# Attention into a gated FFN on one core: one query group's x turned on TensorE, and unread identity products ahead of the first scores

## The chip, the cores and the metric

The kernel runs on one core of a Trainium2 chip. The metric is the device time of one execution in microseconds. The profile is of one execution, taken by the hardware profiler; its engines are named PE (TensorE), PEld (TensorE's weight loads), DVE (VectorE), ACT (ScalarE), POOL (GpSimd) and SP (SyncE, which here only issues DMAs).

## The reference

Eight batches, eight heads, 576 tokens of 64 elements a head, and 16 "beacon" keys and values ahead of each head's own. Attention is causal over the tokens and open to the beacons; its output, with the heads side by side, is the x (4608 tokens by 512) of a gated feed-forward layer.

```python
k_all = np.concatenate([beacon_k, k], axis=2)
v_all = np.concatenate([beacon_v, v], axis=2)
scores = scale * np.matmul(q, k_all.transpose(0, 1, 3, 2))   # causal mask on the tokens
a = np.exp(scores - scores.max(-1, keepdims=True))
a /= a.sum(-1, keepdims=True) + 1e-09
x = np.matmul(a, v_all)          # then (batch, token, head * 64): 4608 x 512
gate = np.maximum(x @ w_gate, 0.0)                           # 512 -> 1536
return (gate * (x @ w_val)) @ w_out                          # 1536 -> 512
```

## The kernel before, in words

**Attention.** A unit of attention is one batch, one pair of heads (four pairs) and one of two query groups: group 0 is the first 368 tokens in three query tiles (112, 128, 128 rows), group 1 the last 208 in two (128, 80). For a unit TensorE makes the scores with keys on the partitions (`qk`, L339; from batch 2 on in slabs over several units, L362), ScalarE takes the exponential (L388; slabs L370 and L372), VectorE multiplies the diagonal blocks with a triangular mask (L400; slabs L379 and L382; GpSimd does it for two units of the very start, L397). `av` (L421) multiplies the weights with v, which carries a column of ones, so that the sum of the weights comes along; VectorE takes the reciprocal (L429) and writes the divided x in bf16, tokens on the partitions (L430).

**Turning.** The FFN needs x with its features on the partitions (`xT`). There are two ways. `x_turn` (L437) issues DMA transposes on SP, one for each query tile, over all four pairs of a group, after the last pair's `av`. `x_turn_pair` (L445, L446) transposes one pair on TensorE, one product with the identity per query tile, into a PSUM bank, and an engine copies the bank into `xT`. Before the change, `x_turn_pair` serves batch 0 alone; batches 1 to 7 use `x_turn`. q and k are turned likewise: for batches 0 and 1 on TensorE (`pair_turn`, L319 and L322, copied out at L325; the beacons' keys at L290), from batch 2 on by DMA transposes on SP (L296), after a load on SP (L254, L255 and their like) and a cast to bf16 on GpSimd (L282). The program puts such a turn behind the next load or two: load at one step, cast two steps on, turn three steps on.

**FFN.** Tokens go in tiles of 368 and 208 (the query groups). For each tile, 12 units `ffn_up`: four products with a block of w_gate (L454), a Relu on ScalarE (L457), four products with a block of w_val (L462), and VectorE's product of the two (L470, `hT`). For each 128 tokens of a finished block of 512, a unit `ffn_down`: 12 products with w_out (L493), a copy on ScalarE (L498), and a store issued by GpSimd (L500).

**Order.** The program is written out by hand, engine by engine in the order of its text; semaphores alone tie the engines together. The start (batch 0's group 0) is spelled out: six small loads of q and k by GpSimd's queue (`cs`), then for each pair `pair_turn`, then `scores` (that is `start`, `qk`, `softmax`), with masks, weight loads (`chunk`, three pieces of w_gate and w_val, L554) and `av` between. From batch 1 on, a loop over steps takes a step's attention units and fills in FFN units up to a budget; the order of FFN units comes from a planner's costs and from when a tile's x is due. In a step, `aver` issues the `av` of the units of the step before, and `passed` issues loads, casts and turns whose time has come; `held` keeps these back while a group's last `av` has not been issued, so that `x_turn`'s transposes stand ahead of them on SP. Each of SP, GpSimd and the compute engines works strictly in its order, so an instruction that waits holds up all behind it.

**PSUM.** Two score tiles take four of the eight banks. The other four form the ring `f`: every other use of PSUM (transposes, `av`, FFN) takes the next bank in turn, and waits until its reader of four uses ago is done.

Of the kernel before, what the change touches and what calls it, by code (L numbers as in the profile page):

```python
# [10 lines left out]
FP32 = mybir.dt.float32  # L11
# [131 lines left out]
def kernel(  # L143
# [15 lines left out]
    P = 128  # L159
# [13 lines left out]
    V, G, A, T = nc.vector, nc.gpsimd, nc.scalar, nc.tensor  # L173

    const = ctx.enter_context(tc.tile_pool(name="const", bufs=1))
    ident = const.tile([P, P], BF16, name="ident")
# [34 lines left out]
    f_ps = Ring("f_ps", 4, space=bass.MemoryType.PSUM)  # L211
# [98 lines left out]
    def pair_turn(c, b, p, part, cps):  # L310
        r0, r1, s0 = PARTS[part]
        n = r1 - r0
        tps = [f_ps.tile([P, n, D], BF16, name="f") for _ in range(2)]
        for r in range(r0, r1):
            for i in range(2):
                rows = slice(i * D, (i + 1) * D)
                if isinstance(c, Load):
                    flat = c.c.rearrange("p a n -> p (a n)")
                    T.transpose(tps[i][:, r - r0], flat[rows, r * P:(r + 1) * P], ident[rows, rows])  # L319
                    continue  # L320
                for a in range(2):
                    T.transpose(tps[i][a * D:(a + 1) * D, r - r0], c[rows, 2 * p + a, r * D:(r + 1) * D],  # L322
                                ident[rows, rows])
        for i in range(2):
            cps[i](kqs[b % 2][:, i, p, Nb + s0:Nb + s0 + n * D].rearrange("q (p r) -> q p r", r=n),  # L325
                   tps[i].rearrange("q r p -> q p r"))
# [4 lines left out]
    def qk(u):  # L331
        u.s, u.p, u.parts = [], [], []
        kq = kqs[u.b % 2]
        for segs, cols, _ in SLABS[u.g]:
            s = s_ps.tile([P, 2, 512], FP32, name="s")
            for (kt, q0, n, c) in segs:
                for a in range(2):
                    rows = slice(a * D, (a + 1) * D)
                    T.matmul(s[:, a, c:c + n], kq[rows, 0, u.pi, kt * P:(kt + 1) * P],  # L339
                             kq[rows, 1, u.pi, Nb + q0:Nb + q0 + n], start=True, stop=True)  # L340
            u.s.append(s)
# [7 lines left out]
    class Slab:  # L349
# [26 lines left out]
        def mask(self):  # L376
            n, m = self.spans
            if n == 1:
                V.tensor_mul(self.p[:, :, :m], self.p[:, :, :m], tri[:, :, :m])  # L379
                return  # L380
            d = self.p.rearrange("p a (s c) -> p (a s) c", s=n)[:, :, :m]
            V.tensor_mul(d, d, tri[:, 0:1, :m].to_broadcast([P, 2 * n, m]))  # L382

    def softmax(u, which=(0, 1)):
        for i in which:
            cols = SLABS[u.g][i][1]
            flat, p = weights(cols)
            A.activation(p, u.s[i][:, :, :cols], AF.Exp, scale=scale)  # L388
            u.p.append(p)
            u.parts.append((flat, cols, SLABS[u.g][i][0]))  # L390
# [43 lines left out]
    def x_turn(u):  # L434
        for qi in QGROUPS[u.g]:
            r0, rn = QROWS[qi]
            nc.sync.dma_start_transpose(xT[:, :, u.b * S + r0:u.b * S + r0 + rn], u.x[:rn, qi, :])  # L437

    def x_turn_pair(u, cp):
        qt = QGROUPS[u.g]  # L440
        c0, c1 = QROWS[qt[0]][0], QROWS[qt[-1]][0] + QROWS[qt[-1]][1]
        tp = f_ps.tile([P, 384], BF16, name="f")
        for qi in qt:
            r0, rn = QROWS[qi]
            T.transpose(tp[:, r0 - c0:r0 - c0 + rn], u.x[:rn, qi, u.pi * P:(u.pi + 1) * P], ident[:rn, :rn])  # L445
        cp(xT[:, u.pi, u.b * S + c0:u.b * S + c1], tp[:, :c1 - c0])  # L446
# [78 lines left out]
    with tc.manual_schedule():  # L525
# [13 lines left out]
        for b in range(B):  # L539
            for p, g in [(p, g) for g in range(2) for p in range(NP)]:  # L540
                u = Burst()
# [3 lines left out]
        def start(u):  # L545
            if u.b not in xs:
                xs[u.b] = xsb.tile([P, NKT, d_model], BF16, name="x")
            u.x = xs[u.b]
# [10 lines left out]

        VV = (V.tensor_copy, V.tensor_copy)  # L560
        VA = (V.tensor_copy, A.copy)
        def scores(u):
            start(u)
            qk(u)
            softmax(u)

# [6 lines left out]
        for p in range(1, NP):  # L573
# [3 lines left out]
        G.affine_select(out=tri[:, :, P:], in_=tri[:, :, P:], pattern=[[0, 2], [1, 240 - P]],  # L577
                        compare_op=ALU.is_ge, fill=0.0, base=Nb, channel_multiplier=-1)

        first.cast(V, A)  # L580
        bk[0].cast(A)
        pair_turn(first, 0, 0, 0, VA)
        bk[0].turn(V.tensor_copy)
        pair_turn(c0, 0, 1, 0, VA)
        g0 = bursts[:NP]
        scores(g0[0])
        mask(g0[0], True)
        chunk(0, 256)
# [28 lines left out]
        ffn = []  # L617
# [7 lines left out]
        def next_ffn(mid=None):  # L625
            ffn.pop(0)[1](mid)
# [35 lines left out]
        while len(ffn) > LEFT:  # L662
            if len(ffn) == LEFT + 1:
                bk[1].turn(V.tensor_copy)
                pair_turn(c1, 1, 0, 2, VA)
            next_ffn()
# [46 lines left out]
        def budget(s):  # L713
            best = W0 if s < 8 else CAP * widths[s]
            for r in sorted(set(ready.values())):
                if r > pos[s]:
                    best = min(best, sum(c for c, _, e in ffn if ready[e] < r) / (r - pos[s]) * widths[s])
            return best

        clock = []  # L720

        def passed(t):
            while clock and clock[0][0] <= t + 1e-6:
                clock.pop(0)[2]()
# [18 lines left out]
        for s, e in enumerate(steps):  # L743
            units = [u for u in last if last[u] == s - 1]
            want += budget(s)

            def fits():
                return ffn and ready[ffn[0][2]] <= pos[s] and spent + ffn[0][0] / 2 <= want

            def held():  # L750
                return any(u.last for u in units)

            def aver():
                if units:
                    u = units.pop(0)
                    av(u)
                    if u.last:
                        x_turn(u)

            if not isinstance(e, list):  # L760
                u = e
                turn = u and u.b == 1 and u.g == 0 and not u.last
                if turn:
                    pair_turn(c1, 1, u.pi + 1, 2, VA)
                late = False
                if u:
                    late = not turn and ffn and ready[ffn[0][2]] <= pos[s] and ffn[0][0] < 1
                    start(u)
                    qk(u)
                    softmax(u, (0,) if late else (0, 1))  # L770
                while units:
                    aver()
                passed(pos[s])
                rest = []
                if late:
                    rest = [lambda: (softmax(u, (1,)), mask(u, which=(0,))), lambda: mask(u, which=(1,))]
                elif u:
                    mask(u)
                while fits():
                    spent += ffn[0][0]  # L780
                    next_ffn()
                    if rest:
                        rest.pop(0)()
                for f in rest:
                    f()
                continue
            for i, sl in enumerate(e):
                for u, _ in sl.segs:
                    start(u)
                sl.qk([f_ps.tile([P, 512], FP32, name="f") for _ in range(2)] if i == 0 else  # L790
                      s_ps.tile([P, 2, 512], FP32, name="s"))
            exps, masks = list(e), []

            def exp():
                if exps:
                    sl = exps.pop(0)
                    sl.exp()
                    masks.append(sl)

            exp()  # L800
            aver()
            if not held():
                passed(pos[s])
            gone, was, room = 0.0, spent, max(want - spent, 0.1)
            while fits():
                c = ffn[0][0]
                gone += c
                mid = gone >= STEP
                if mid:
                    gone = 0.0  # L810
                old = len(masks)
                next_ffn(exp if mid else None)
                spent += c
                if old:
                    masks.pop(0).mask()
                if mid:
                    aver()
                if not held():
                    passed(pos[s] + widths[s] * min((spent - was) / room, 0.99))
            while exps:  # L820
                exp()
            while units:
                aver()
            for sl in masks:
                sl.mask()
        assert not clock
        while ffn:
            if len(ffn) == 10:
                range_flags()
# [38 lines left out]
```

## Time and profile before

| | |
|---|---|
| Time, median of 4 runs | 377.61 us (376.09 to 378.18) |
| The profiled execution's own time | 375.27 us |
| Its span, first to last instruction | 373.5 us |
| TensorE busy / ScalarE / VectorE / GpSimd | 95% / 55% / 51% / 24% |
| DMA transposes of x on SP | 35, median 3.3 us from issue to landing |
| TensorE transposes of x (L445) | 20 |
| Copies of turned x (L446) | 4 on ScalarE (368 columns), 4 on VectorE (208 columns) |

Spans are of one execution, and the numbers that a view gives are of that one; the median belongs to other executions of the same kernel. In a timeline a line gives the start, the time from the start of the first to the end of the last instruction merged into it, engine, line, operation, output<-input, shape and count, and in brackets the idle time of the engine before it with what ended it. Products overlap: their pace is read from start to start, not from the length of one. "DMA xT<-x" names the landing of a transfer. In a wait list the three numbers are the total, the times and the longest.

### The profile page before, as it was taken

Reading aid. Unit: us, or ns where it says so; the run is one execution under the profiler, and the core shown is the slowest. Engines: PE = TensorE matmul, PEld = TensorE weight load, DVE = VectorE, ACT = ScalarE, POOL = GpSimd, SP = SyncE. Lnnn points to the kernel's source line nnn. Section 1 sums busy time; section 2 is a strip of 40 time slices with the busy share of each in tenths; the row PEclk is TensorE's granted clock in tenths of the full one; section 3 lists DMA queues with packets and bytes.
Section 4 is the critical chain, followed back from the end, with each engine's and each line's share of the span. In section 5 each row is a group of like instructions: output and inputs, shape, how many; then the busy total and the mean of one; then the engine's idle time right before and its main releaser. Section 6 shows DMA issues by size and latency. Waiting matters only on the chain.

```text
span 373.5 us, 9601 instructions
## 1 busy us (share of the span) xinstructions
PE 356.5 (95%) x3757; PEld 238.3 (64%) x3757; DVE 190.7 (51%) x630; ACT 204.3 (55%) x388; POOL 89.3 (24%) x126
## 2 busy tenths in 40 slices
PE   3799989999998999999999999999999999999995
PEld 2556666567745686565596657865596647865763
DVE  3657367457424674365365643564566625552230
ACT  5665366656555664555466554655565736632322
POOL 6962033321142112311321323111321011000100
PEclk9999999999999999999999999999999999999999
DMA  8999999999999887975868969878685021101202
GB/s 150 188 202 207 212 205 193 194 194 127 161 221 194 154 153 133 212 169 97 211 138 147 157 148 236 127 164 158 155 143 100 16 65 65 35 16 38 84 32 90
DMA packets 156947, 53.12 MB, mean 142 GB/s; under 512 B 146528, under 2 KB 154464, under 8 KB 156896
## 3 DMA queue, kind: packets, MB, share of 16 engines
q1 hardware_dynamic: 145088, 36.72, 56.5%
q0 software_dynamic: 11376, 15.27, 18.9%
q8 instruction: 31, 0.51, 0.6%
q10 hardware_dynamic: 432, 0.46, 0.4%
q14 instruction: 20, 0.16, 0.2%
HBM read 38.47 MB, written 9.44 MB: 128 GB/s over the span
## 4 chain that ended last, share of the span: by engine, by line
PE 87%; DMA 4%; SPq 2%; ACT 2%; DVE 1%; POOL 1%; issue 1%; POOLq 0%; ACTq 0%; DVEq 0%
PE f L454 24%; PE f L462 24%; PE f L493 22%; PE f L421 9%; PE s L362 3%; PE f L362 2%; PE s L339 2%; DMA cs<-in_q_dram 2%; DMA stg<-in_q_dram 2%; DMA kq<-c 1%; SPq L296 1%; POOL cs L308 1%; ACT p L388 1%; PE f L481 1%; DVE hT L470 1%
## 5 line engine op out<-in xcount | busy, mean ns | idle before, releaser
L470 DVE TENSOR_TENSOR hT<-g,f 128x208 bf16<-128x208 f32 (+14 forms) x288 | 92.8, 351 | 86.8 <-PE f L462 54.7
L454 PE MATMUL f<-xT,wg 128*128 128x368 bf16 (+1 forms) x768 | 125.9, 286 | 1.6 <-DMA xT<-x 1.0
L462 PE MATMUL f<-xT,wv 128*128 128x368 bf16 (+1 forms) x768 | 125.6, 286 | 0.9 <-DVE hT L470 0.8
L457 ACT ACTIVATE g<-f 128x368 f32<-128x368 f32 (+1 forms) x192 | 78.9, 414 | 78.5 <-PE f L454 41.9
L493 PE MATMUL f<-wo,hT 128*128 128x512 bf16 x420 | 94.7, 379 | 0.1
L462 PEld LDWEIGHTS <-wv 128*128 128x128 bf16 x768 | 71.0, 98 | 26.0 <-DVE hT L470 1.1
L454 PEld LDWEIGHTS <-wg 128*128 128x128 bf16 x768 | 69.6, 98 | 23.0 <-issue 3.3
L493 PEld LDWEIGHTS <-hT 128*128 128x128 bf16 x420 | 39.9, 98 | 44.2
L498 ACT COPY ob<-f 128x512 f32<-128x512 f32 x35 | 20.5, 585 | 65.5 <-PE f L493 57.8
L372 ACT ACTIVATE p<-s 128x992 bf16<-128x992 f32 (+2 forms) x56 | 53.8, 966 | 0.0
L282 POOL CAST c<-stg 128x1024 bf16<-128x1024 f32 (+1 forms) x30 | 31.2, 1041 | 88.9 <-DMA stg<-in_q_dram 86.3
L500 POOL DMA_DIRECT2D out_dram<-ob x32 | 17.3, 542 | 132.5 <-ACT ob L498 123.3
L429 DVE RECIPROCAL rall<-f 128x2 f32<-128x2 f32 (+1 forms) x96 | 16.6, 173 | 63.3 <-PE f L421 62.5
L421 PEld LDWEIGHTS <-p 128*128 128x128 bf16 (+2 forms) x960 | 36.1, 101 | 10.6 <-issue 6.2
L421 PE MATMUL f<-vx,p 128*128 128x65 bf16 (+2 forms) x960 | 41.5, 197 | 0.8 <-DVE p L400 0.8
L430 DVE TENSOR_TENSOR x<-f,rall 128x128 bf16<-128x128 f32 (+1 forms) x96 | 36.3, 378 | 3.5
L370 ACT ACTIVATE p<-f 128x496 bf16<-128x496 f32 (+2 forms) x56 | 28.7, 567 | 7.6 <-PE f L362 7.6
L388 ACT ACTIVATE p<-s 128x992 bf16<-128x992 f32 (+2 forms) x32 | 26.1, 867 | 5.0 <-PE s L339 4.9
L379 DVE TENSOR_TENSOR p<-p,tri 128x160 bf16<-128x160 bf16 (+1 forms) x72 | 28.6, 401 | 0.4 <-ACT p L372 0.4
L269 POOL CAST vx<-stg 128x1024 bf16<-128x1024 f32 (+2 forms) x21 | 18.9, 899 | 30.2 <-DMA stg<-in_v_dram 14.8
L362 PEld LDWEIGHTS <-kq 64*128 64x128 bf16 x384 | 13.9, 94 | 10.5 <-issue 9.4
L362 PE MATMUL s<-kq 64*128 64x208 bf16 (+4 forms) x256 | 16.2, 249 | 0.7 <-DMA kq<-c 0.7
(58 smaller groups left out, 108.9 us busy)
## 6 DMA issues: line engine op xcount, KB each, us to landing
out_dram<-ob POOLq DMA_DIRECT2D x32, 256.0 KB, 3.2
stg<-in_v_dram SPq DMA_DIRECT2D x24, 256.0 KB, 5.3
stg<-in_k_dram SPq DMA_DIRECT2D x18, 256.0 KB, 4.2
stg<-in_q_dram SPq DMA_DIRECT2D x18, 256.0 KB, 5.0
stg<-in_v_dram SPq DMA_DIRECT2D x8, 224.0 KB, 4.2
wo<-in_moe_w_out_dram POOLq DMA_DIRECT2D x3, 512.0 KB, 14.1
stg<-in_k_dram SPq DMA_DIRECT2D x6, 224.0 KB, 3.9
stg<-in_q_dram SPq DMA_DIRECT2D x6, 224.0 KB, 4.4
```

The costliest lines, as they stand in the source:

```text
L282: cp(self.c[:n], self.st[:n])
L362: T.matmul(o[:, c:c + n], kq[rows, 0, u.pi, kt * P:(kt + 1) * P], kq[rows, 1, u.pi, Nb + q0:Nb + q0 + n], start=True, stop=True)
L370: A.activation(p[:, a], self.s[a][:, :self.cols], AF.Exp, scale=scale)
L372: A.activation(p, self.s[:, :, :self.cols], AF.Exp, scale=scale)
L388: A.activation(p, u.s[i][:, :, :cols], AF.Exp, scale=scale)
L421: T.matmul(o[:m, j, a, 0:D + 1], p[:kr, c:c + m], vs[u.b % 2][:kr, kt, 2 * u.pi + a, 0:D + 1], start=first, stop=(kt == kts[-1]), skip_gro ...
L430: V.tensor_mul(u.x[:m, i0:i0 + j1 - j0, u.pi * P:(u.pi + 1) * P].rearrange("p j (a d) -> p j a d", a=2), o[:m, j0:j1, :, 0:D], r.unsqueeze ...
L454: T.matmul(g[:, :mn], wg[:, ki, nf * P:(nf + 1) * P], xT[:, ki, m0:m0 + mn], start=(ki == 0), stop=(ki == KM - 1))
L457: A.activation(gs[:, :mn], g[:, :mn], AF.Relu)
L462: T.matmul(u[:, :mn], wv[:, ki, nf * P:(nf + 1) * P], xT[:, ki, m0:m0 + mn], start=(ki == 0), stop=(ki == KM - 1))
L470: V.tensor_mul(hbs[i][:, nf, c - i * HB:e - i * HB], gs[:, c - m0:e - m0], u[:, c - m0:e - m0])
L493: T.matmul(o, hbs[i][:, nf, ms * P:(ms + 1) * P], wo[:, nf, :], start=(nf == 0), stop=(nf == NF - 1))
```

## The change

Two things are added. First, a function `keep_busy` that makes n products of the 128x128 identity with itself into one bank of the ring `f`, which nothing reads: 30 of them ahead of the first transposes, and 8 ahead of the scores of each of pairs 1, 2 and 3 of batch 0's group 0. Second, x of batch 2's group 0 is turned pair by pair by `x_turn_pair` with VectorE's copy, in place of the three DMA transposes of `x_turn`: a pair is noted after its `av`, and turned once two FFN units have been issued after that.

```diff
+        def keep_busy(n):
+            ps = f_ps.tile([P, P], FP32, name="f")
+            for _ in range(n):
+                T.matmul(ps, ident, ident, start=True, stop=True)
+
         def scores(u):
             start(u)
+            if u.g == 0 and u.pi:
+                keep_busy(8)
             qk(u)
             softmax(u)
...
+        keep_busy(30)
         first.cast(V, A)
         bk[0].cast(A)
         pair_turn(first, 0, 0, 0, VA)
...
-        clock = []
+        clock, unturned = [], []
...
+            def turn_pair():
+                if unturned and unturned[0][1] > len(ffn) + 1:
+                    x_turn_pair(unturned.pop(0)[0], V.tensor_copy)
+
...
                     av(u)
-                    if u.last:
+                    if (u.b, u.g) == (2, 0):
+                        unturned.append((u, len(ffn)))
+                    elif u.last:
                         x_turn(u)
...
                 next_ffn(exp if mid else None)
+                turn_pair()
                 spent += c
...
-        assert not clock
+        assert not clock and not unturned
```

In the built program TensorE gets 54 identity products and 12 transposes more, VectorE 4 copies of 368 columns more (the first two behind the second and the fourth FFN unit after the first pair's `av`, the last between the two `ffn_down` units ahead of the tile that reads it), and SP three DMA transposes less. Nothing else changes its place on any engine.

## The prediction

> **What bounds the kernel now.** I read the page first, then what TensorE waited for, then its timeline where those waits lie, then SP's queue and GpSimd over the same microseconds.
>
> The page's first lines:
>
> ```profile
> span 373.5 us, 9601 instructions
> PE 356.5 (95%) x3757; PEld 238.3 (64%) x3757; DVE 190.7 (51%) x630; ACT 204.3 (55%) x388; POOL 89.3 (24%) x126
> ```
>
> TensorE is busy 95% of the span, 17.0 us short of it. An edit gains only by shortening TensorE's work or by closing one of its gaps, and adds its own TensorE time in full wherever TensorE is otherwise dense. TensorE's waits (total us, times, longest us):
>
> ```profile
> PE f L319 <- ACT c L279: 5.6, 1, 5.6
> PE s L339 <- ACT p L388: 1.3, 2, 0.9
> PE f L454 <- DMA xT<-x: 1.0, 1, 1.0
> PE f L322 <- DMA cs<-in_q_dram: 0.8, 1, 0.8
> PE s L362 <- DMA kq<-c: 0.7, 1, 0.7
> ```
>
> First, second and fourth lie before 14 us, where the products go. The third is the one place where an x tile comes too late from the DMA transposes. TensorE's timeline there (start, us, instruction, idle before it):
>
> ```profile
> 106.51 5.34 PE L493 MATMUL f<-wo,hT 128*128 128x512 bf16 x24
> 112.90 0.78 PE L454 MATMUL f<-xT,wg 128*128 128x368 bf16 x4 [1.05 <-DMA xT<-x]
> ...
> 116.76 0.44 PE L362 MATMUL s<-kq 64*128 64x128 bf16 x4 [0.71 <-DMA kq<-c]
> ```
>
> Batch 2's first 368 tokens begin at 112.90 after 1.05 us idle; 3 us later the scores of batch 3 wait 0.71 us for kq. SP's queue, and the cast that the later kq needs:
>
> ```profile
> 101.25 3.04 SPq L296 DMA_TRANSPOSE kq<-c  x2
> ...
> 105.75 5.24 SPq L437 DMA_TRANSPOSE xT<-x  x3
> 111.10 2.53 SPq L296 DMA_TRANSPOSE kq<-c  x2
> ```
>
> ```profile
> 103.00 1.04 POOL L282 CAST c<-stg 128x1024 bf16<-128x1024 f32 x1 [3.06 <-DMA stg<-in_q_dram]
> ```
>
> SP issues in program order. Counting casts and turns in the program, the pair at 111.10 reads the tile cast at 103.00 to 104.04: it was ready 7 us earlier and stood behind the three x transposes. (The chain of waits says otherwise: it goes from 116.76 through the cast at 110.73. That cast feeds the next pair, at 115.79; I take the program's order over that inference.) So x's 5.24 us on SP cause both waits, 1.05 + 0.71 = 1.76 us.
>
> **The turns, TensorE.** Twelve transposes, 368 columns a pair. Nearest row: the two at 32.03 (128 + 80 columns) let the next product start at 32.13, so 0.10 us for 208 columns, 0.18 for 368, 0.71 for four pairs. Three pairs stand among dense products, the last between two down products (L493) ahead of 112; all 0.71 is paid. The Trainium skill speaks against this: "TensorE: Matmul & The Clock Gate", section "Part 4: PE-mode transpose", gives about 275 ns for one 128x128 transpose inside a kernel. Twelve of those make 3.3 us, more than the 1.76 us to be won, and the edit would lose 1.5. But that is one's duration (here too a record lasts some 0.26 us); in a stream the row's 0.05 us each counts. I take 0.71; ends 0.6 and 3.3, near the first.
>
> **The turns, VectorE and the ring.** Four copies of 368 columns out of PSUM; 208 columns took 0.26 (32.80), so about 0.45 each. The last two fall where VectorE idles over 2 us and cost nothing. The first two stand in its queue between the hT products (L470) of 90 to 94 us; there VectorE is busy 3.69 of 4.50 us. Behind them wait the division of the next pair's x and the hT products that free banks of the four-bank ring. A backlog of 0.9 us has the idle 0.67 before 94.0 and about 0.28 before each product after it, so it is gone by 96. Bounds: nothing, and 1.4 us for each of the two (backlog, drain and copy on the path); no gain is possible here. I take 0.1, as TensorE shows no wait for VectorE there now.
>
> **The turns, SP.** Three issues go. The kq pair starts near 105.7 instead of 111.10, so its kq lands four or five us earlier and the 0.71 closes. The last x is divided by 103.6, its turn follows the first of two down products, near 109.2, and its copy ends by 110: the 1.05 closes too. The loads behind that pair move up as well, into the time that the three transposes held; no TensorE wait in this region stands on them. Next to be late is the second query group's xT of batch 2, which landed at 132.97 for the products at 133.39; SP issues it at 128.05, over 1 us after its x is ready, and would now reach it in time. Sum for the turns: -1.76 + 0.71 + 0.1 = -0.95 us.
>
> **The thirty products.** They need only ident, ready on GpSimd at 1.39. Three transposes of 368 columns took 0.29 us at 15.77, so 0.10 for 128 columns at that pace; thirty take 3.0 and end near 4.5, inside the 5.64 us in which TensorE waits for the first cast. Cost nothing; were that cast early, at most the overlap. What they may bring is the clock. The page's row of it, then TensorE's timeline:
>
> ```profile
> PEclk9999999999999999999999999999999999999999
> ```
>
> ```profile
> 13.79 2.16 PE L421 MATMUL f<-vx,p 128*128 128x65 bf16 x36
> ...
> 18.09 1.19 PE L454 MATMUL f<-xT,wg 128*128 128x368 bf16 x4
> 19.11 0.79 PE L462 MATMUL f<-xT,wv 128*128 128x368 bf16 x4
> ...
> 117.13 0.74 PE L421 MATMUL f<-vx,p 128*128 128x65 bf16 x18
> ```
>
> The clock row shows full speed in every slice, but the paces differ: 36 products in 1.98 us (start at 13.79 to the next start at 15.77) is 55 ns, against 0.58 / 18 = 32 ns at 117; four 368-column products take 1.02 at 18.09 and 0.62 from 19.11. So TensorE runs at about half pace until nearly 19 us, five us into its first dense stretch.
>
> **The three times eight.** At half pace 0.81, at full pace (0.48 ns a column) 0.49 each. The first fills the 0.41 us gap before 8.91; the rest is eaten by the 0.83 us wait for cs, landed at 10.78. The third fills the 0.88 us gap before 12.97. The second finds no gap: the scores at 11.29 follow their transposes at once, and ScalarE waits for them (0.89 at 11.93), so all of it delays the third and fourth exponentials, the mask on GpSimd and the last pair's av. At full pace 0.49 less some 0.25 for the faster transposes and scores, less 0.15 before the fourth exponential: about +0.1. Then the two last av, the turn and the products gain 0.6 to 0.7, so the first value product (19.11) comes near 18.5. But the next weights bound that: wv's second chunk landed at 23.00 for a product at 23.51, the third at 28.32 for one at 28.89, and that queue is full. So -0.3 us is kept, -0.5 at most. At half pace throughout: +0.8 at the third scores, +0.6 at 19 us.
>
> The skill speaks against full pace. "TensorE: Matmul & The Clock Gate", section "What's actually happening": the clock opens after about 3.4 us of sustained work, measured in a window that runs free of the kernel. Thirty products are 3.0 us with over 1 us idle behind, so no full window unless the measure tolerates gaps; by the rule alone this term is nearer +0.6. The trace shows a release after 5.1 us of work with gaps of up to 0.27 in it, so some tolerance; and with the gaps filled, work is unbroken from 10.8 on, three us sooner than before, which takes the loss back to about nothing even if the first thirty fail. I take -0.3 as nearest the case with released clock; ends -0.5 and +0.6.
>
> **Sum.** -0.95 - 0.3 = -1.25 on the profiled execution's 375.27 us (span 373.5 and 1.8 around it): 374.0. It lies 2.34 below the median of the runs shown; the same change on the median gives 376.4.
>
> **Rivals.**
> - *More is won* (chance 0.22). The median run loses 2.3 us that this profile doesn't show. Only transfers here vary so: the load issued at 104.95 took 5.63 us where the median is 5.0. If half of that loss is later xT and kq at 112 to 117, some 1.2 more closes: 375.2. Against it: the loss can as well lie in the weights before 40 us.
> - *Another wait takes the place* (0.20). If the chain of waits is right and the kq pair really waits for the cast at 110.73, kq lands at 116.7 as before. TensorE, arriving 1.05 - 0.81 earlier, waits that much longer; the turns bring nothing, and the start between -0.3 and +0.6. 377.5. Program order speaks against it.
> - *The ring stops TensorE, slower* (0.08). Each of the first two turns takes a bank that comes free only behind VectorE's queue. At 1.4 us each the sum is -1.76 + 0.71 + 2.8 - 0.3 = +1.45: 379.1. It decides from 1.35 us of TensorE idle between 89 and 96, where it has almost none now.
> - *The likeliest* as summed, 0.50: 376.4, its own range 375.5 to 377.2.
>
> **Numbers.** A measurement of this kernel can tell about 0.5% (1.9 us) from no change. Faster by more, under 375.7: most of the first rival and a tail of the likeliest, 0.27. Slower by more, over 379.5: half of the ring's case, 0.04. Within: 0.69. The range takes in the first rival's case and the second's with the run's own spread (376.09 to 378.18 before), and leaves out the ring: 374.5 to 378.1.
>
> **What would show it.** No TensorE wait for xT at 112 nor for kq at 116; SP's kq pair at about 105.7; no new TensorE wait for VectorE at 90 to 96. Early: L421's 36 products in 1.2 us instead of 2.0, and the first L462 near 18.5. Wrong if kq still lands at 116.7, if L421 keeps 55 ns, if TensorE stops for wv at 23 or 28 by more than it gained, or if a later wait (xT at 133, kq at 177 with 0.4 us to spare) takes the gain back.

## The result and the profile after

| | before | after |
|---|---|---|
| Median (lowest to highest, runs) | 377.64 us (374.52 to 380.81, 63) | 375.79 us (374.02 to 377.71, 42) |
| Ratio, 95% interval | | 0.9954 (0.9941 to 0.9966), 1.7 us less |
| The profiled execution's own time | 375.27 us | 375.87 us |

The prediction was 376.4 us (374.5 to 378.1). The gain is on the edge of the 0.5% named there, and the whole interval lies below 1. The two profiled executions say the opposite of the medians: that of after took 0.6 us more. So the profiles are good for single steps, not for the total.

The first lines of the page of after:

```profile
span 373.9 us, 9730 instructions
PE 360.9 (97%) x3823; PEld 241.9 (65%) x3823; DVE 193.4 (52%) x634; ACT 204.6 (55%) x388; POOL 90.1 (24%) x126
```

TensorE is busy 4.4 us more in a span 0.4 us longer: work was added and idle time taken away. Its waits in after (total, times, longest):

```profile
PE f L565 <- POOL ident masks.py:199: 1.4, 1, 1.4
PE f L462 <- DVE hT L470: 1.4, 4, 0.5
PE f L319 <- ACT c L279: 0.8, 1, 0.8
PE f L290 <- ACT c L274: 0.8, 1, 0.8
PE f L445 <- DVE x L430: 0.8, 3, 0.4
PE f L462 <- DMA wv<-in_moe_w_val_dram: 0.5, 1, 0.5
...
PE f L454 <- DMA wg<-in_moe_w_gate_dram: 0.4, 1, 0.4
```

The waits for xT and for kq are gone. The 5.6 us for the first cast have become 0.8 because the thirty products fill them. New are the two waits for weights; they are not peculiar to the identity products, as turns only below shows. TensorE where xT and kq were late:

```profile
107.30 2.75 PE L493 MATMUL f<-wo,hT 128*128 128x512 bf16 x12
109.89 0.33 PE L445 MATMUL f<-ident,x 112*128 112x112 bf16 x3
110.06 2.75 PE L493 MATMUL f<-wo,hT 128*128 128x512 bf16 x12
112.65 0.79 PE L454 MATMUL f<-xT,wg 128*128 128x368 bf16 x4
...
115.46 0.55 PE L362 MATMUL s<-kq 64*128 64x208 bf16 x8
```

No brackets: nothing is waited for. The last pair's three transposes start at 109.89 and let the next product start at 110.06: 0.17 us. SP's queue over the same stretch:

```profile
106.37 0.58 SPq L254 DMA_DIRECT2D stg<-in_k_dram  x1
107.00 0.74 SPq L255 DMA_DIRECT2D stg<-in_q_dram  x1
107.85 3.30 SPq L296 DMA_TRANSPOSE kq<-c  x2
```

The kq pair follows the loads directly; it landed at 112.69 and 113.15, for scores at 115.46. It starts at 107.85 and not at the 105.7 of the prediction because SP as a whole is 2 us later here: the pair before it starts at 103.31, where it was 101.25.

The start of after:

```profile
1.45 3.38 PE L565 MATMUL f<-ident 128*128 128x128 bf16 x30 [1.45 <-POOL ident masks.py:199]
...
8.86 1.04 PE L565 MATMUL f<-ident 128*128 128x128 bf16 x8
...
11.03 1.04 PE L565 MATMUL f<-ident 128*128 128x128 bf16 x8
12.00 0.81 PE L339 MATMUL s<-kq 64*128 64x128 bf16 x6
12.74 0.74 PE L565 MATMUL f<-ident 128*128 128x128 bf16 x8
13.69 0.77 PE L339 MATMUL s<-kq 64*128 64x128 bf16 x6 [0.20 <-ACT p L388]
14.39 1.26 PE L421 MATMUL f<-vx,p 128*128 128x65 bf16 x36
...
18.07 1.03 PE L454 MATMUL f<-xT,wg 128*128 128x368 bf16 x4
18.94 0.78 PE L462 MATMUL f<-xT,wv 128*128 128x368 bf16 x4
...
23.15 0.80 PE L454 MATMUL f<-xT,wg 128*128 128x368 bf16 x4 [0.38 <-DMA wg<-in_moe_w_gate_dram]
24.48 0.80 PE L462 MATMUL f<-xT,wv 128*128 128x368 bf16 x4 [0.53 <-DMA wv<-in_moe_w_val_dram]
```

The first two eights took 0.97 us each (start to the next start), which is half pace; full pace came within the third. In the trace's record of the granted clock full speed begins at 13.0 us, in before at 18.9. L421's 36 products took 1.3 us instead of 2.0. Still the first FFN product starts at 18.07, where it was 18.09 before: what the faster products gained, the scores of pairs 3 and 4 had lost by starting 0.7 later, and TensorE now waits 0.8 us for VectorE's division of x (L430) where it waited 0.3. Then the third FFN unit stops for both its weights: they are issued at 16.23 instead of 15.72 and land at 23.10 and 24.43 instead of 21.67 and 23.00. Whether the later issue is the cause is taken up under "The weights".

### The profile page after: what moved, and what is told of

Same layout as the page of the kernel before. It is cut to its first block, busy times and chain, and to the rows that moved or that the text cites. A ratio compares the mean times of both kernels' runs of the same rounds, so it can differ in the third digit from the quotient of the medians.

```text
span 373.9 us, 9730 instructions
## 1 busy us (share of the span) xinstructions
PE 360.9 (97%) x3823; PEld 241.9 (65%) x3823; DVE 193.4 (52%) x634; ACT 204.6 (55%) x388; POOL 90.1 (24%) x126
## 4 chain that ended last, share of the span: by engine, by line
PE 91%; DMA 3%; ACT 2%; DVE 1%; issue 1%; POOL 0%; SPq 0%; DVEq 0%; ACTq 0%
PE f L462 25%; PE f L493 24%; PE f L454 24%; PE f L421 9%; PE s L362 3%; PE f L362 2%; DMA wv<-in_moe_w_val_dram 2%; PE s L339 2%; DMA stg<-in_beacon_k_dram 1%; ACT p L388 1%; PE f L322 1%; DVE hT L470 1%; PE f L481 1%; PE f L565 1%; DVE p L400 0%
## 5 line engine op out<-in xcount | busy, mean ns | idle before, releaser
L498 ACT COPY ob<-f 128x512 f32<-128x512 f32 x35 | 20.5, 586 | 65.8 <-PE f L493 57.7
L421 PEld LDWEIGHTS <-p 128*128 128x128 bf16 (+2 forms) x960 | 34.8, 99 | 10.2 <-issue 6.0
L421 PE MATMUL f<-vx,p 128*128 128x65 bf16 (+2 forms) x960 | 40.5, 194 | 0.6 <-DVE p L400 0.5
L430 DVE TENSOR_TENSOR x<-f,rall 128x128 bf16<-128x128 f32 (+1 forms) x96 | 36.3, 378 | 3.4
L379 DVE TENSOR_TENSOR p<-p,tri 128x160 bf16<-128x160 bf16 (+1 forms) x72 | 31.4, 439 | 0.4 <-ACT p L372 0.4
```

Of the source, the lines that this page charges most:

```text
L421: T.matmul(o[:m, j, a, 0:D + 1], p[:kr, c:c + m], vs[u.b % 2][:kr, kt, 2 * u.pi + a, 0:D + 1], start=first, stop=(kt == kts[-1]), skip_gro ...
L430: V.tensor_mul(u.x[:m, i0:i0 + j1 - j0, u.pi * P:(u.pi + 1) * P].rearrange("p j (a d) -> p j a d", a=2), o[:m, j0:j1, :, 0:D], r.unsqueeze ...
```

## The experiments

Every ratio is against the kernel before on the same chip, measured in turn with it. The runs are told in the order of what they settle.

### The two parts by themselves

*turns only*: the change without its identity products.

```diff
-            if u.g == 0 and u.pi:
-                keep_busy(8)
...
-        keep_busy(30)
```

> The changed kernel without any identity product; x of batch 2's first group is turned on TensorE. If the turns carry the gain (the two waits at 112 and 116 us close, 0.7 us of transposes is paid), the ratio to before is 0.9965 +- 0.001 (-1.0 to -1.5 us). If the products carry it, the ratio is 1.000. If the two add up, this and the products-only kernel together give the whole 0.9954. In the trace: 36 products of L421 in 2.0 us, first L462 at 19.1, no wait for xT at 112, none for kq at 116.

Measured: 0.9956 (0.9939 to 0.9972), as much as the whole change. Neither xT nor kq is waited for. At the start its third FFN unit stops for weights much as that of after does, without any identity product:

```profile
22.61 0.80 PE L454 MATMUL f<-xT,wg 128*128 128x368 bf16 x4 [0.16 <-DMA wg<-in_moe_w_gate_dram]
23.91 0.80 PE L462 MATMUL f<-xT,wv 128*128 128x368 bf16 x4 [0.51 <-DMA wv<-in_moe_w_val_dram]
```

*products only*: all 54 products, x of the group by SP's transposes as before.

```diff
-                    if (u.b, u.g) == (2, 0):
-                        unturned.append((u, len(ffn)))
-                    elif u.last:
+                    if u.last:
                         x_turn(u)
```

> The changed kernel with all identity products and with the DMA transposes of x as before. If the weights' arrival at 23 to 29 us takes back what the faster clock gives, the ratio is 0.999 to 1.000; if the clock's gain of 0.3 to 0.6 us is kept, 0.9985; if the products explain what the result has over my sum, 0.997. In the trace the clock is released by 9 to 13 us, and TensorE waits for wg or wv at 23 to 29; the waits at 112 and 116 are there as before.

Measured: 1.0034 (1.0014 to 1.0055). Its waits of TensorE for what SP transposes:

```profile
PE f L454 <- DMA xT<-x: 2.8, 2, 1.5
...
PE s L362 <- DMA kq<-c: 0.7, 1, 0.7
```

The wait at 112 (1.5 us) and that for kq are there as in before. A second wait for xT, 1.3 us, stands at 135.33, at batch 2's second query group, which the prediction had named as next to be late.

So the turns carry the gain. The products alone lose, and beside the turns they neither gain nor lose.

### Is it SP's time, or TensorE's way of turning?

*turns twice*: the whole change, and SP's three transposes put back. They read x and write a buffer that nothing reads, so TensorE doesn't need them.

```diff
                     if (u.b, u.g) == (2, 0):
                         unturned.append((u, len(ffn)))
+                        if u.last:
+                            spare = csb.tile([P, H, R * D], BF16, name="cs")
+                            for qi in QGROUPS[u.g]:
+                                r0, rn = QROWS[qi]
+                                nc.sync.dma_start_transpose(spare[:, :KM, r0:r0 + rn], u.x[:rn, qi, :])
```

> The changed kernel, with the three DMA transposes of x put back on SP's queue at their old place; they write a free buffer that nothing reads, x itself still comes from TensorE. If SP's order alone makes kq late (the pair of kq turns stands behind the three), its wait of 0.7 to 1.0 us at 116 comes back, no wait for xT does, and the time lies 0.7 to 1.1 us above the changed kernel (ratio to before 0.9975). If kq is late because of its cast at 110.7, as the chain of waits has it, the changed kernel and this one have the same wait and the same time (0.9954).

Measured: 1.0038 (1.002 to 1.0055), the same as with products only and x by DMA. After, which differs from it in these three transposes alone, has 0.9954 in its own series: that is 3.2 us less, where 0.7 to 1.1 were expected. SP's queue in this kernel:

```profile
106.67 4.19 SPq L775 DMA_TRANSPOSE cs<-x  x3
110.98 2.65 SPq L296 DMA_TRANSPOSE kq<-c  x2
```

TensorE in this kernel:

```profile
115.48 0.44 PE L362 MATMUL s<-kq 64*128 64x128 bf16 x4 [0.30 <-DMA kq<-c]
...
133.78 0.52 PE L454 MATMUL f<-xT,wg 128*128 128x208 bf16 x4 [1.51 <-DMA xT<-x]
```

Three transposes that nobody uses take back all that the turns win. kq is late again because its pair is issued behind them (110.98, as 111.10 in before) and not because it moves more slowly: the pair's second transpose took 3.2 us from issue to landing here and 3.4 in after. The wait for xT at 133, which was not expected, has two parts: its first transpose is issued 1.1 us later than in after (127.49 for 126.38) and holds SP for 3.3 us instead of 1.8, so the second, on which the wait ends, lands at 133.65 instead of 132.00. These waits are 1.8 of the 3.2 us; where the rest lies was not seen. So the gain comes from what the three transposes hold up by being on SP, not from the way in which x is turned. How much of their cost is SP's issue time and how much what they move through the DMA engines was not separated; for kq the order alone suffices, as the next experiment shows.

### SP's order alone

*kq ahead*: the kernel before, with the three x transposes of that group put behind the kq pair instead of ahead of it. No turn on TensorE, no products, the same load on SP.

```diff
+        def kq_turn(x):
+            x.turn()
+            if behind:
+                x_turn(behind.pop())
...
-                    at(t + TD, n - 99, x.turn)
+                    at(t + TD, n - 99, lambda: kq_turn(x))
...
-                    if u.last:
+                    if (u.b, u.g, u.last) == (2, 0, True):
+                        behind.append(u)
+                    elif u.last:
                         x_turn(u)
```

> The kernel before, with no turn on TensorE and no identity products; the three DMA transposes of batch 2's first group stand on SP behind the pair that turns q and k instead of ahead of it. SP's load is the same, the order alone is other. If the order is what made kq late (the prediction's reading), the wait for kq at 116 is gone, x lands about 2.5 us later and the wait for it at 112 grows to about 3.5 us: 1.003 to 1.006 of before. If kq waits for its cast (the second rival), that pair still starts after 110.7 with the x transposes behind it, and both waits are there.

SP and TensorE in this kernel:

```profile
104.27 3.10 SPq L296 DMA_TRANSPOSE kq<-c  x2
107.47 5.16 SPq L437 DMA_TRANSPOSE xT<-x  x3
```

```profile
114.38 0.80 PE L454 MATMUL f<-xT,wg 128*128 128x368 bf16 x4 [2.61 <-DMA xT<-x]
...
117.20 0.55 PE L362 MATMUL s<-kq 64*128 64x208 bf16 x8
```

The pair starts at 104.27, and the cast that before's chain of waits names runs at 109.91 in this kernel: the pair never waited for it. The chain of waits had the wrong cause and the program's order the right one. The wait for kq is gone and that for xT has grown from 1.05 to 2.61 (3.5 was expected). The measured ratio is 1.0137 (1.0097 to 1.0177), more than twice the largest loss expected. It rests on only six executions. The profiled one is the fastest (376.23 us, mean granted clock 1.000); the other five took 380.1 to 383.5 with a mean clock of 0.984 to 0.995. That fits a wait long enough to lose the clock, which the next experiments show at another place; where these five lost it was not seen.

### The products, part by part

*thirty only* is the kernel before with nothing but the thirty products.

```diff
+        keep_busy(30)
         first.cast(V, A)
```

> Only the thirty products ahead of the first transposes; no eights, x turned by DMA as before. If the thirty alone release the clock (a window that tolerates gaps), the first L421 run at 32 ns and the second eight's cost (about 0.5 us on the way to the third exponential) is saved: first L462 near 18.0, ratio 0.998 to 0.999. If the eights are needed for the release, it comes at 19 us as before, L421 keeps 55 ns, ratio 1.000.

*second eight* is the kernel before with nothing but the eight ahead of pair 2, *other eights* that with the eights ahead of pairs 1 and 3.

```diff
             start(u)
+            if u.g == 0 and u.pi == 2:
+                keep_busy(8)
             qk(u)
```

> The kernel before, with only the eight products ahead of pair 2's scores, which has no gap on TensorE. If all of the eight lies on the way to the third and fourth exponential, the mask on GpSimd and the weight loads behind it, the second weight chunk is issued 0.6 to 0.8 us later and lands as much later, ratio 1.001 to 1.003. If that queue is full anyway, as I predicted, nothing beyond the 20 us mark moves: 1.000.

```diff
             start(u)
+            if u.g == 0 and u.pi in (1, 3):
+                keep_busy(8)
             qk(u)
```

> The kernel before, with the eights ahead of pairs 1 and 3 only, which fill gaps of 0.41 and 0.88 us. By the gaps they cost at most 0.4 us ahead of a wait for cs and nothing at the third: ratio 1.000. If any eight delays the weights, 1.001 to 1.003 as for pair 2.

*turns and thirty* is the change without its eights, *turns and two eights* the change without the thirty and the second eight.

```diff
-            if u.g == 0 and u.pi:
-                keep_busy(8)
```

> The changed kernel without the three eights: turns on TensorE and the thirty products. If the eights cost what the products-only kernel lost and the thirty are free, this is the best of the family: ratio 0.994 to 0.9955. If the eights cost nothing once SP has slack behind the turns, it equals the changed kernel and the turns alone, 0.9955.

```diff
-            if u.g == 0 and u.pi:
+            if u.g == 0 and u.pi in (1, 3):
                 keep_busy(8)
...
-        keep_busy(30)
```

> The change with only the products ahead of pairs 1 and 3: the thirty and the eight ahead of pair 2 are left out. Ahead of pairs 1 and 3 alone, on the kernel before, the first FFN product came 0.55 us earlier in the profile and the time was 1.0001 (0.9974 to 1.0028). If the weights at 23 to 26 us take back whatever the start gains, this equals the turns alone: 0.9956 of before, no wait for xT or kq, and a wait for wg or wv of 0.5 us or more. If the thirty and the second eight cost what the other two gain, it is below that: 0.994, with the first FFN product near 17.5 and the later groups still ahead.

| kernel | ratio (95%) | full clock from | first FFN product | sixth FFN unit | xT wait at 70 to 73 |
|---|---|---|---|---|---|
| before | 1 | 18.9 | 18.09 | 30.79 | none |
| turns only | 0.9956 (0.9939 to 0.9972) | 16.9 | 17.75 | 31.09 | none |
| kq ahead | 1.0137 (1.0097 to 1.0177) | 16.8 | 17.47 | 30.43 | none |
| after | 0.9954 (0.9941 to 0.9966) | 13.0 | 18.07 | 31.66 | none |
| products only | 1.0034 (1.0014 to 1.0055) | 12.6 | 18.16 | 30.93 | none |
| turns twice | 1.0038 (1.002 to 1.0055) | 13.4 | 18.27 | 31.02 | none |
| thirty only | 0.9982 (0.996 to 1.0004) | 5.3, lost 8.8 to 19.0 | 18.05 | 30.82 | 0.20 |
| second eight | 1.0008 (0.9988 to 1.0027) | 19.1 | 18.63 | 31.21 | 1.30 |
| other eights | 1.0001 (0.9974 to 1.0028) | 10.6 | 17.54 | 30.87 | 1.07 |
| turns and thirty | 0.9993 (0.9971 to 1.0015) | 20.5 | 18.86 | 32.28 | 0.26 |
| turns and two eights | 0.9993 (0.9967 to 1.0019) | 15.2 | 17.82 | 30.94 | 0.73 |

Starts and waits are in us, each of one execution. Three things are to be seen. First, the clock comes earlier in all five kernels that have the eights ahead of pairs 1 and 3 (10.6 to 15.2, against 16.8 to 18.9 in the three without products). The thirty brought it in one profiled execution of five, and it was lost again. Second, the first FFN product doesn't follow the clock. The three kernels without products start it at 17.47 to 18.09, the three with all of them at 18.07 to 18.27, the two with the eights of pairs 1 and 3 alone at 17.54 and 17.82. The second eight by itself gives 18.63; it finds no gap, as the prediction had worked out. Third, at the sixth unit all but two stand between 30.43 and 31.21 whatever they did before.

The mean recorded clock of every execution tells more about the thirty. It takes the time before the first record as full speed, so only a clock that was granted and lost again lowers it: the profiled thirty only, with 10.24 us at half speed after its early release, has 0.984. It is 0.991 or less in 15 of the 22 executions of thirty only and in 8 of the 14 of turns and thirty, but in 3 of 173 of before. So the thirty probably bring full speed early, for a while, in more than half of the executions. Those are not faster: their median in thirty only is 375.55 us, that of the others 375.65.

Three expectations failed here. Turns and thirty and turns and two eights were expected at 0.994 to 0.9956, and both gave 0.9993. In second eight the second weight piece was to be issued and to land 0.6 to 0.8 us later; it was issued 0.54 later and landed 0.1 later.

### The weights

*the same, finer chunk* is turns and two eights, with the second weight piece loaded in halves. *turns, finer chunk* has the same split and no products; its expectation is the second one below.

```diff
-        chunk(256, 512)
+        chunk(256, 384)
+        chunk(384, 512)
```

> The same two eights and the turns, and the second piece of w_gate and w_val (columns 256 to 512, which the third and fourth FFN units read) loaded as two pieces of 128 columns. If the arrival of that piece is what takes the start's gain back, TensorE's waits for wg and wv at 23 to 26 us shrink by up to 1 us and the ratio lies 0.001 to 0.002 below that of the run without the split. If the four smaller loads land no earlier (more issues on the same queue), both are equal, and the wait moves to a later unit.

> The turns and the split loads, with no identity products at all. Beside the run with the two eights and the same split it tells what the eights are worth when the weights don't bound the start: about 0.5 us (0.0015) if the release of the clock is worth what the first FFN product showed, nothing if the gain goes elsewhere. Beside the turns alone (0.9956) it tells what the split by itself does: nothing, if the start without the eights isn't bound by these weights.

Measured: 0.9999 (0.998 to 1.0019) and 0.9963 (0.9945 to 0.9981). TensorE in the one with products, the fourth unit and the fifth:

```profile
25.05 0.78 PE L454 MATMUL f<-xT,wg 128*128 128x368 bf16 x4
...
29.05 0.80 PE L462 MATMUL f<-xT,wv 128*128 128x368 bf16 x4 [0.58 <-DMA wv<-in_moe_w_val_dram]
```

And the fifth unit in the one without:

```profile
29.20 0.80 PE L462 MATMUL f<-xT,wv 128*128 128x368 bf16 x4 [0.68 <-DVE p L400]
```

With halves the waits at 22 to 26 are gone in both, and the wait has moved to the fifth unit at 29. (The second view names VectorE; that wv landed at 29.15, 0.05 before the product, so it was the transfer there too.) Turns and two eights, unsplit, has its fifth unit's wv at 28.99. The last of these pieces lands at 29.0 to 29.15 in all three, halves or not, products or not (28.32 in before). So in these kernels the start is bound by when the weights have come in, and an earlier first product cannot be kept. Over all 14 profiled executions this last piece lands between 28.2 and 30.0.

Does a product ahead of the weights' issue make them late? The runs don't show it. Turns only issues the second piece of w_gate at 15.50, earlier than before (15.72), and it lands at 22.56, later than in before (21.67). Second eight issues it at 16.26, later than after (16.23), and it lands at 21.76, where after's takes until 23.10. Over the twelve profiled executions that load this piece whole, issues at 15.39 to 16.43 land at 21.10 to 23.10 with little relation between the two. What moves the landing stays open.

Why the kernel with products and halves is 1.1 us slower than that without products (medians 376.66 and 375.56) is not explained by this. Its profiled execution took 380.58 us, one of four in 22 above 378, so it shows a rare case: it lost its time elsewhere. Its TensorE, and then, for three stretches, the busy time of TensorE, its weight loads, VectorE, ScalarE and GpSimd, the granted clock, the DMA share (a packet counts where it starts, so it can exceed 1) and GB/s:

```profile
73.46 1.38 PE L454 MATMUL f<-xT,wg 128*128 128x368 bf16 x4 [3.64 <-DMA xT<-x]
74.64 1.43 PE L462 MATMUL f<-xT,wv 128*128 128x368 bf16 x4
...
79.62 0.79 PE L454 MATMUL f<-xT,wg 128*128 128x368 bf16 x4
```

```profile
68.00:72.00 4.00, 1.82 (x31) 1.04 (x29) 1.26 (x6) 2.24 (x3) 1.52 (x2) 0.98 1.33 167
72.00:78.50 6.50, 5.04 (x18) 2.25 (x20) 0.54 (x1) 0.95 (x2) 1.04 (x1) 0.50 0.87 186
78.50:84.00 5.50, 5.50 (x72) 3.91 (x72) 4.32 (x13) 3.08 (x5) 1.09 (x1) 0.98 1.11 194
```

x of batch 1's first query group, which this change doesn't touch, comes 3.64 us late, and from 71.9, within that wait, the granted clock stands at 0.50 for 6.8 us: two FFN units on, this execution is 5.4 us behind before, having been 0.2 ahead at 55. That transfer is close in every kernel: the last of its three pieces landed 0.13 to 0.46 us before its product in the seven executions that didn't wait, and from issue to landing it took between 2.8 and 6.2 us.

### Loads taken off SP

*v on GpSimd*: the kernel before, with the loads of v from batch 2 on issued by GpSimd.

```diff
-            dma = nc.sync.dma_start
+            dma = G.dma_start if self.kind == "v" and self.key[0] > 1 else nc.sync.dma_start
```

> The kernel before, with the loads of v of batches 2 to 7 issued by GpSimd instead of SP; the same bytes move, x is turned by DMA on SP. If SP's issue time bounds 64 to 135 us (each batch's v loads hold SP some 3 to 4 us), SP reaches the x transposes earlier, the waits for xT and kq shrink, ratio 0.994 to 0.997. If the DMA engines' throughput bounds there, moving the issue changes nothing: 0.999 to 1.001. If loads stuck behind a waiting cast on GpSimd make v late, slower: above 1.002.

Measured: 1.0052 (1.002 to 1.0083). That is the number of the third case but not its cause: TensorE nowhere waits for v. The wait for kq at 116 is gone, but x of batch 1's first group is late again:

```profile
72.89 1.39 PE L454 MATMUL f<-xT,wg 128*128 128x368 bf16 x4 [2.87 <-DMA xT<-x]
```

Half clock sets in within this wait too, from 72.4 for 3.4 us. The third x transpose took 6.2 us from issue to landing, where it took 3.7 in before. Taking issues from SP was not enough by itself; whether the loads, landing at other times, slowed that transpose was not told apart.

## Why the prediction was right, and where not

**The turns: right in kind, too small.** Its term for the turns was -0.95 us; turns alone measured 0.9956 of 376.98, -1.7 us, with 0.6 either way. Three terms, from the same stretch of both profiles (39th FFN unit to the 51st, 26.55 us in before and 24.90 in after):
- *The waits, -1.76.* From start to start the down products before 112 took 11.67 us in before and 10.45 in after, the scores 2.39 and 1.46: 1.22 + 0.93 = 2.15 us. A wait list counts from the modelled end of the last product; the stop also breaks the overlap of the products, about 0.2 us each time. This term was mis-sized by 0.4.
- *TensorE's transposes, 0.71.* The nine in this stretch took 0.50, so twelve take 0.67. The row at 32.03 decided rightly between its 0.05 us each and the 275 ns of the Trainium skill ("TensorE: Matmul & The Clock Gate", "Part 4: PE-mode transpose"); twelve of those would have made 3.3 us and a loss. The row is of before:

```profile
32.03 0.26 PE L445 MATMUL f<-ident,x 128*128 128x128 bf16 x2
32.13 0.63 PE L454 MATMUL f<-xT,wg 128*128 128x368 bf16 x3
```

- *VectorE and the ring, 0.1.* Every other kind of product takes the same time in both, to 0.02 us. No stop in this stretch: nearly nothing.

That makes -2.15 + 0.67 = -1.48 in the profiles, and the median's -1.7 agrees with it within its interval. The agreement leans on one execution of before. In the profiled thirty only and second eight, SP's program is that of before and TensorE waits neither at 112 nor at 116; this is thirty only, whose x landed at 111.18:

```profile
111.82 0.79 PE L454 MATMUL f<-xT,wg 128*128 128x368 bf16 x4
```

They wait elsewhere (see the first rival below), so what the turns win is an average over executions that lose it at different places. The ring's rival, 1.35 us of idle at 89 to 96, didn't happen.

**The cause: right.** Program order on SP, not the cast. Kq ahead moves the pair by a change of order alone, and turns twice brings the wait back with transposes that nobody reads. The second rival falls.

**The first rival, more is won: in part.** Of before's 63 executions a third took over 378 us, of after's 42 none. One execution of before was profiled, so the places were not seen. Among the seven profiled that turn this group's x by DMA, the waits for xT and kq together come to between 0.2 and 3.5 us, at 70, 112, 116 or 133. Five of the other six wait at a place where before's profile shows none. The mean recorded clock points the same way. In 41 of 173 executions of before it is 0.992 to 0.996, about one step of 3.41 us at half speed, as v on GpSimd has (0.995) for its wait of 2.87 us. In the series with turns only these are 17 of before's 75, with a median 1.2 us above that of the executions at 0.997 or more; of turns only it is 2 of 22. Among the executions at 0.997 or more the turns win 1.5 us (375.07 against 376.60), close to the 1.48 of the profiles; so part of the rest is probably that fewer executions lose the clock.

**The products, -0.3: not found.** Beside the turns they bring nothing (0.9954 and 0.9956), with some 0.8 us either way, which doesn't exclude -0.3; without the turns they cost 1.3 us (1.0034), which does. Three steps of the working failed.
- *The price.* "With the gaps filled, work is unbroken from 10.8 on, three us sooner" was right on the clock, six us sooner, but the first two eights were by then paid at half pace, and at 0.97 us each instead of 0.81. The bound for half pace, +0.8 at the third scores, was the nearer one (12.00 for 11.29).
- *The release.* The Trainium skill's rule ("TensorE: Matmul & The Clock Gate", "What's actually happening") asks for about 3.4 us of sustained work. The prediction read some tolerance from the trace and was right in that: the thirty span only 3.38 us, yet in the profiled thirty only full speed is recorded at 5.34, when TensorE had stood still since 4.83, and the mean clocks say the same of more than half of that kernel's executions. But that release was lost after 3.41 us, and in the other four profiled executions with the thirty full speed came at 12.6 us or later. A release by the thirty that lasts, which -0.3 was nearest to, was not seen.
- *The weights.* Their landings at 23.00 and 28.32 were taken as fixed. They differ between executions by 2 us, with and without products. What was said of them as a bound, that they limit any gain, holds: the halves only moved the stop to 29. In after TensorE stops for them by 0.91 us, more than the 0.17 won at the first value product, which is one of the signs of being wrong that the prediction named.

**The sum: in part luck.** That -1.25 lies within half a microsecond of -1.7 is helped by two errors that pull opposite ways: the turns won 0.75 us more than predicted, the products 0.3 less.

**Next to be late.** xT at 133 was named, and is late in products only, turns twice and second eight. xT at 70 was not named: before's list shows no wait there, and its slack of 0.28 us was not looked at.

**Open.** With each ratio taken against before in its own series: with turns, part of the products costs 0.0037 (thirty, two eights) against turns alone, all of them nothing; without turns, all of them cost 0.0034, part of them nothing. No sum of parts gives that. The six profiled executions with part of the products all wait for xT at 70 to 73 (0.20 to 3.64 us), the three with all of them and the four without products and with v's loads on SP never. So the products may decide by their timing how transfers meet before 70; one execution each doesn't prove it. Turning batch 1's first group on TensorE as well, which would take that wait away, was not tried.

## What to carry to other kernels

On a queue that issues in order, price a step by what stands behind it: three DMA transposes cost TensorE nothing of themselves, and 1.7 us (3.2 with the products beside them) through what they held up, while the same work on a busy TensorE cost 0.67. Where a list shows no wait, look at the slack as well; a transfer that lands 0.3 us early in one execution can be late in another. Before speeding up a start, find the transfer that the first dense stage needs: here the last of these weights land between 28.2 and 30.0 us whatever is done ahead of them. And before explaining a late transfer by a late issue, look for an execution with the one and without the other.

## What the runs showed of the hardware that was not expected

**A long wait costs twice.** Within TensorE waits of 2.87 and 3.64 us the granted clock fell to 0.50, for 3.4 and 6.8 us; over one of 2.61 us it stayed at 1.00. In the record it changes only in steps of 3.41 us.

**VectorE's mask stands still while GpSimd casts.** VectorE, GpSimd and TensorE in after:

```profile
226.13 1.05 POOL L269 CAST vx<-stg 128x1024 bf16<-128x1024 f32 x1
228.86 1.42 DVE L379 TENSOR_TENSOR p<-p,tri 128x160 bf16<-128x160 bf16 x1
...
229.12 1.05 POOL L282 CAST c<-stg 128x1024 bf16<-128x1024 f32 x1
...
230.62 0.52 PE L462 MATMUL f<-xT,wv 128*128 128x208 bf16 x4 [0.49 <-DVE hT L470]
```

The same mask in before, with no cast beside it:

```profile
230.04 0.23 DVE L379 TENSOR_TENSOR p<-p,tri 128x160 bf16<-128x160 bf16 x1
```

0.23 us became 1.42, about the cast's 1.05 more, and TensorE lost 0.49 for it. In before the same happens elsewhere (1.32 and 1.50 us at 158 and 182). There 19 masks begin while a cast runs: 18 end 0.09 to 0.28 us after that cast's end, and one, the 1.32, runs on into the next cast. A mask that begins just before a cast is held in some cases and not in others. VectorE's instructions that read PSUM are not held: beside a cast `hT` (368 columns) and the division of x keep their 0.54 and 0.56 us. Which masks meet a cast differs between executions; how much of the difference in time comes from there was not measured.
